# Half of the last 1 MB of output weights loaded by a transfer of 125 partitions

## The chip, the cores and the metric

The kernel runs on one core of one Trainium2 chip. The metric is device time in microseconds (us) of that core. Repeated runs of one kernel agree within about 0.2%.

## The reference

One decode step of a transformer block, batch 8, one token each: layer norm with modulation from a conditioning vector `c`, grouped-query attention over a cache of 8192 keys (32 query heads, 8 key/value heads of 128), output projection, and a squared-ReLU MLP.

```python
def _A_ref(x, k_cache, v_cache, wq, wo):          # x: 8 x 1 x 512
    q = (x @ wq).reshape(B, Sq, Hq, Dh)...         # 32 heads of 128
    scores = einsum('bhqd,bhkd->bhqk', q, k) * Dh ** -0.5
    o = einsum('bhqk,bhkd->bhqd', softmax(scores), v)
    return o.reshape(B, Sq, Hq * Dh) @ wo          # wo: 4096 x 512
...
x = x + ga * _A_ref(h, A_k_cache, A_v_cache, A_wq, A_wo)
h = _layernorm(x) * (1 + cb) + sb
x = x + gb * _B_ref(h, B_w1, B_b1, B_w2, B_b2)
```

Keys and values are 268 MB of bf16. Everything else is small: `wo` is 4 MB.

## The kernel before

A helper records operations per engine and adds the semaphores. All large loads are issued from SyncE into one queue. Four ring slots of 4 MB take two key or value heads each; a slot is loaded again when its reader is done.

```python
def load(n):                                   # 64 loads of 4 MB, 128 partitions x 32 KB
    ...
    loaded[n] = dma("sync", s_ring[s], lambda e: e.dma_start(slot(s), src), dep)
...
load(0)
load(1)
...                                            # b1, b2
wo_e = wo_sb[:, 0:24, :].rearrange("p (g j) n -> p g (j n)", j=4)
d_woe = dma("sync", s_woe, lambda e: e.dma_start(
    wo_e, A_wo[0:24 * DH, :].rearrange("(g p j) n -> p g (j n)", g=6, p=128)))   # 3 MB, rows of 4 KB
d_wo = dma("sync", s_wo, lambda e: e.dma_start(
    wo_sb[:, 24:32, :], A_wo[24 * DH:, :].rearrange("(h dh) n -> dh h n", dh=DH)))  # 1 MB, rows of 1 KB
load(2)
load(3)
...                                            # 8 batches: transpose keys, scores, softmax, values
```

At the very end `w1` (two transfers) and `w2` (four) are loaded by the same queue into a free ring slot, behind the last values. The last matmuls of the MLP wait for the last of them.

Of the kernel before, what the change touches and what calls it, by code (L numbers as in the profile page):

```python
# [30 lines left out]
class Prog:  # L31
# [27 lines left out]
    def dma(self, eng, sem, fn, deps=()):  # L59
        self.dma_n[sem] = self.dma_n.get(sem, 0) + 16  # L60
        self.ops[eng].append(Op(fn, deps, None, sem, self.at))
        return Tok(sem, None, self.at, self.dma_n[sem])
# [90 lines left out]
def bass_adaLN_cond__gqa_block_cached__dense_activation_squared_relu__decode_kernel(  # L153
    nc, A_x, A_k_cache, A_v_cache, A_wq, A_wo, B_x, B_w1, B_b1, B_w2, B_b2, c, w_mod, out):
    B, _, D = A_x.shape
    _, HKV, SK, DH = A_k_cache.shape
# [14 lines left out]
    with ExitStack() as es:  # L171
# [4 lines left out]
        wo_sb = sb("wo_sb", [128, HQ, D], BF16)  # L176
# [72 lines left out]
        op, dma = Pg.op, Pg.dma  # L249
        sem = lambda name: E(nc.semaphore(name))  # L250
        s_c, s_x, s_wm, s_wq, s_woe, s_wo, s_bb = (
            sem(f"d_{n}") for n in ("c", "x", "wm", "wq", "woe", "wo", "bb"))
# [68 lines left out]
        def load(n):  # L321
            kv, b, p = units[n]
            s = n % NSLOT
            src = (A_k_cache if kv == "k" else A_v_cache)[b, 2 * p:2 * p + 2]
            src = src.rearrange("g s d -> (g s d)").rearrange("(p f) -> p f", p=128)
            dep = [released.get(s)]
            if units[n] == last:
                t0, toks = 0, []
                for i, t1 in enumerate(CH):
                    toks.append(dma("sync", s_last[i], lambda e, a=t0 * DH, z=t1 * DH: e.dma_start(  # L330
                        RING[:, s, a:z], src[:, a:z]), dep))
                    t0 = t1
                loaded[n] = toks
            else:
                loaded[n] = dma("sync", s_ring[s], lambda e: e.dma_start(slot(s), src), dep)
# [54 lines left out]
        for g in range(HKV):  # L390
# [14 lines left out]
        wo_e = wo_sb[:, 0:24, :].rearrange("p (g j) n -> p g (j n)", j=4)  # L405
        d_woe = dma("sync", s_woe, lambda e: e.dma_start(
            wo_e, A_wo[0:24 * DH, :].rearrange("(g p j) n -> p g (j n)", g=6, p=128)))
        d_wo = dma("sync", s_wo, lambda e: e.dma_start(
            wo_sb[:, 24:32, :], A_wo[24 * DH:, :].rearrange("(h dh) n -> dh h n", dh=DH)))
        load(2)  # L410
        load(3)
        next_load = NSLOT
# [68 lines left out]
        for b in range(B):  # L481
# [4 lines left out]
            for p in range(NP):  # L486
                n = 2 * NP * b + p
# [65 lines left out]
            for p in range(NP):  # L553
                n = 2 * NP * b + NP + p
# [180 lines left out]
```

## Time and profile before

| | before |
|---|---|
| time, median (range) | 670.66 us (670.59 to 670.72) |
| span of the profiled run | 668.8 us |
| TensorE busy | 74% |
| DMA busy, by slices | 90% or more in 39 of 40 slices |
| bytes moved | 283.95 MB, 425 GB/s on average |

From the page of before: the busy share of TensorE and of the DMA engines in tenths, in 40 slices of the span, and what the DMA engines moved.

```profile
PE   2394964799639983699647996399846996489976
...
DMA  9999999999999999999999999999999999999996
GB/s 375 430 404 427 431 427 437 434 425 433 433 433 427 432 433 435 431 429 429 435 435 425 434 433 432 427 431 433 439 433 423 428 439 435 421 433 435 437 408 259
```

TensorE has gaps everywhere, the DMA engines have none: the loads set the pace. From the DMA issues of before (size of each, time from issue to landing):

```profile
ring<-in_A_k_cache_dram SPq DMA_DIRECT2D x32, 4096.0 KB, 34.9
...
wo_sb<-in_A_wo_dram SPq DMA_DIRECT2D x1, 3072.0 KB, 45.4
...
wo_sb<-in_A_wo_dram SPq DMA_DIRECT2D x1, 1024.0 KB, 47.9
```

A 4 MB load takes 9.7 us when its turn has come (the distance between successive landings). Key loads land 35 us after their issue, value loads 28 us (medians), so two to three others are queued ahead of each. (SPq is SyncE's queue, which issues the transfers; "issue" is time in which an engine waited for nothing that the profile shows.) The end of the chain of waits of before (start, length, what):

```profile
649.68 1.45 SPq L602
651.13 0.05 issue
651.18 14.19 DMA ring<-in_B_w_dram
665.38 0.05 issue
665.42 0.39 PE PS L685 x8
```

The last slice of `w2` lands at 665.38 us, and about 3.4 us of work follow. Four stretches around the loading of the 1 MB. The columns are the stretch, its length, the busy time and count of PE (TensorE's matmuls), PEld (its weight loads), DVE (VectorE), ACT (ScalarE) and POOL (GpSimd), then the TensorE clock, the busy share of the DMA engines and GB/s.

```profile
44.00:48.00 4.00, 4.00 (x68) 2.94 (x66) 2.58 (x4) 2.72 (x3) 0.00 (x0) 1.00 1.03 394
48.00:52.00 4.00, 4.00 (x70) 3.26 (x71) 2.99 (x5) 2.20 (x4) 0.00 (x0) 1.00 1.16 423
52.00:56.00 4.00, 0.39 (x8) 0.00 (x0) 0.28 (x1) 0.91 (x1) 0.00 (x0) 0.98 1.08 461
56.00:60.00 4.00, 0.00 (x0) 0.00 (x0) 0.00 (x0) 0.00 (x0) 0.00 (x0) 0.50 1.00 426
```

The trace also holds two raw lists that the argument rests on: each DMA packet's start, duration and size (a packet is here one row of a transfer, as in the 8192 packets of 32 KB for 64 transfers of 4 MB; there is no engine number), and the landing records, the semaphore increments of a transfer. Each 4 MB load has 16 of them. They are read here as one from each of the 16 DMA engines as it finishes. Each comes with a packet of 4 bytes (before has 1242 of these in the main queue), so the queue's packet count on a page also tells how many landings there were. The spread of the 16 says how far the engines are out of step.

| last slice of w2 | first engine lands | last engine lands | spread |
|---|---|---|---|
| before | 661.64 us | 665.38 us | 3.74 us |

The last engine is the one that matters. The chain above ends at its landing.

### The profile page before, as it was taken

What the parts mean: (1) busy time and instruction counts of PE and PEld (TensorE: products, weight loads), DVE (VectorE), ACT (ScalarE), POOL (GpSimd) and SP (SyncE); (2) the same over time, 40 slices, a digit from 0 to 9 for tenths busy, and PEclk for the clock granted to TensorE, in tenths of its full rate; (3) what the DMA queues carried; (4) which work ended last, traced back from release to release, by engine and by line L of the source; (5) the groups of instructions that cost most, each with busy time, mean ns of one, the idle gap of its engine ahead of it and who ended that gap; (6) DMA issues with size and microseconds to landing.
All of it is one profiled execution on the core that took longest, in us unless ns stands there. A gap on an engine that the chain in (4) does not pass through costs nothing.

```text
span 668.8 us, 16189 instructions
## 1 busy us (share of the span) xinstructions
PE 495.9 (74%) x7492; PEld 341.4 (51%) x7492; DVE 298.8 (45%) x567; ACT 235.1 (35%) x280; POOL 16.9 (3%) x66
## 2 busy tenths in 40 slices
PE   2394964799639983699647996399846996489976
PEld 2383731676318751477316762287414772167634
DVE  2162741466316661267414672166613673156722
ACT  2061630365106640166204660056402662046600
POOL 7200000000000000000000000000000000000000
PEclk9996995699869997699967997589966999689986
DMA  9999999999999999999999999999999999999996
GB/s 375 430 404 427 431 427 437 434 425 433 433 433 427 432 433 435 431 429 429 435 435 425 434 433 432 427 431 433 439 433 423 428 439 435 421 433 435 437 408 259
DMA packets 12969, 283.95 MB, mean 425 GB/s; under 512 B 1266, under 2 KB 2323, under 8 KB 4372
## 3 DMA queue, kind: packets, MB, share of 16 engines
q1 hardware_dynamic: 12900, 283.65, 99.1%
q8 instruction: 13, 0.21, 0.1%
q14 instruction: 8, 0.07, 0.0%
q10 hardware_dynamic: 48, 0.02, 0.0%
HBM read 283.66 MB, written 0.01 MB: 424 GB/s over the span
## 4 chain that ended last, share of the span: by engine, by line
PE 50%; DMA 39%; DVE 5%; ACT 2%; SPq 2%; issue 1%
DMA ring<-in_A_k_cache_dram 37%; PE PS L429 36%; PE PS L444 9%; DVE Pm L533 3%; PE PS L561 2%; DMA ring<-in_B_w_dram 2%; SPq L602 2%; ACT KTb L434 1%; ACT P_sb L511 1%; DVE m L449 1%; PE PS L520 1%; PE PS L420 1%; PE PS L540 0%; DVE rhs_r L537 0%; DVE Dm L502 0%
## 5 line engine op out<-in xcount | busy, mean ns | idle before, releaser
L434 ACT ACTIVATE KTb<-PS 128x1024 bf16<-128x1024 bf16 x192 | 196.7, 1024 | 375.9 <-PE PS L429 375.9
L429 PE MATMUL PS<-IDENT,ring 128*128 128x128 bf16 x4096 | 267.3, 227 | 51.6 <-DMA ring<-in_A_k_cache_dram 51.6
L429 PEld LDWEIGHTS PS<-IDENT,ring 128*128 128x128 bf16 x4096 | 246.7, 102 | 100.3 <-DMA ring<-in_A_k_cache_dram 53.6
L436 DVE COPY KTb<-PS 128x1024 bf16<-128x1024 bf16 x320 | 210.2, 688 | 151.6 <-PE PS L429 149.2
L561 PE MATMUL PS<-ring,Pm 128*32 128x512 bf16 x992 | 83.3, 495 | 63.2 <-DMA ring<-in_A_v_cache_dram 62.3
L570 DVE CAST O_sb<-PS 128x512 bf16<-128x512 f32 x31 | 21.4, 692 | 144.5 <-PE PS L561 144.5
L444 PE MATMUL PS<-KTb,Qb 128*32 128x512 bf16 x1024 | 79.1, 386 | 4.5 <-ACT KTb L434 4.5
L561 PEld LDWEIGHTS PS<-ring,Pm 128*32 128x32 bf16 x992 | 29.5, 116 | 101.9 <-DMA ring<-in_A_v_cache_dram 63.6
L420 PE MATMUL PS<-IDENT 128*128 128x512 bf16 x120 | 31.3, 380 | 0.0
L574 PEld LDWEIGHTS PS<-SEL,O_sb 128*128 128x128 bf16 x124 | 5.3, 99 | 45.3 <-DVE O_sb L570 45.3
L511 ACT ACTIVATE P_sb<-PS,negm 128x512 bf16<-128x512 f32 x32 | 21.6, 686 | 18.9 <-DVE negm L507 18.9
L574 PE MATMUL PS<-SEL,O_sb 128*128 128x8 bf16 x124 | 8.0, 170 | 24.8 <-DVE O_sb L570 24.8
L444 PEld LDWEIGHTS PS<-KTb,Qb 128*32 128x32 bf16 x1024 | 15.4, 94 | 21.1 <-ACT KTb L434 8.5
L533 DVE COPY Pm<-PS 64x512 bf16<-64x512 bf16 x48 | 19.5, 419 | 13.4 <-PE PS L520 12.4
L449 DVE TENSOR_REDUCE m<-PS 128x1 f32<-128x512 f32 x32 | 22.1, 689 | 6.6 <-PE PS L444 6.6
L520 PE MATMUL PS<-IDENT,P_sb 128*64 128x128 bf16 x512 | 20.4, 222 | 2.0 <-ACT P_sb L511 1.2
L520 PEld LDWEIGHTS PS<-IDENT,P_sb 128*64 128x64 bf16 x512 | 15.2, 109 | 9.8 <-ACT P_sb L511 9.8
L420 PEld LDWEIGHTS PS<-IDENT 128*128 128x128 bf16 x120 | 9.9, 103 | 10.8 <-issue 3.4
L577 DVE TENSOR_TENSOR oTn<-PS,rinv 128x8 bf16<-128x8 f32 x31 | 6.0, 194 | 10.9 <-PE PS L574 10.9
L530 ACT ACTIVATE Pm<-PS 64x512 bf16<-64x512 bf16 x16 | 9.5, 593 | 1.1
L386 PE MATMUL PS<-haT,ring 128*128 128x8 bf16 x128 | 3.6, 168 | 7.6 <-DMA ring<-in_A_wq_dram 7.6
L668 ACT ACTIVATE std<-PS,epst 128x8 f32<-128x8 f32 x1 | 0.3, 268 | 25.1 <-PE PS L667 25.1
(112 smaller groups left out, 98.8 us busy)
## 6 DMA issues: line engine op xcount, KB each, us to landing
ring<-in_A_k_cache_dram SPq DMA_DIRECT2D x32, 4096.0 KB, 34.9
ring<-in_A_v_cache_dram SPq DMA_DIRECT2D x31, 4096.0 KB, 28.2
ring<-in_A_wq_dram SPq DMA_DIRECT2D x1, 4096.0 KB, 20.6
ring<-in_w_mod_dram SPq DMA_DIRECT2D x1, 3072.0 KB, 10.6
wo_sb<-in_A_wo_dram SPq DMA_DIRECT2D x1, 3072.0 KB, 45.4
ring<-in_A_v_cache_dram SPq DMA_DIRECT2D x1, 2048.0 KB, 23.6
ring<-in_B_w_dram SPq DMA_DIRECT2D x3, 512.0 KB, 17.5
ring<-in_B_w_dram SPq DMA_DIRECT2D x1, 1344.0 KB, 21.1
```

What stands on the lines that cost most here:

```text
L420: op("tensor", lambda e: e.matmul(bank(at).rearrange("p (a r) -> p a r", a=4), IDENT[:, :], rhs))
L429: t = op("tensor", lambda e, j=j, i=i: e.matmul(STG[j][:, i, :], src[:, 32 * k + 8 * j + i, :], IDENT[:, :], is_transpose=True), [loaded[n ...
L434: stg_free[j] = op("scalar", lambda e, j=j, dst=dst: e.activation(dst, STG[j], ACT.Copy), [t], "scaP")
L436: stg_free[j] = op("vector", lambda e, j=j, dst=dst: e.tensor_copy(dst, STG[j]), [t], "vecP")
L444: t = op("tensor", lambda e, hf=hf, q=q, rhs=rhs: e.matmul(PS[32 * q:32 * (q + 1), k, :], Qb[:, 2 * p + hf, :], rhs, start=(p == 0 and hf ...
L449: return op("vector", lambda e: e.tensor_reduce(m4[:, k:k + 1], bank(k), AX.X, ALU.max), [t])
L511: exps.append(op("scalar", lambda e, k=k: e.activation(P_sb[:, k, :], bank(k), ACT.Exp, bias=negm[:, 0:1], scale=inv_sqrt, accum_out=rs4[: ...
L520: t = op("tensor", lambda e, k=k, i=i, hf=hf, src=src: e.matmul(STG[k][64 * hf:64 * (hf + 1), i, :], src, IDENT[:, :], is_transpose=True, ...
L533: done.append(op("vector", lambda e, dst=dst, frm=frm: e.tensor_copy(dst, frm), [t, k_pm], "vecP"))
L561: t = op("tensor", lambda e, p=p, m=m, cg=cg, vt=vt, Obank=Obank: e.matmul(Obank[32 * cg:32 * (cg + 1), :], lhs[:, p, 32 * m:32 * m + 32], ...
L570: t = op("vector", lambda e, osb=osb, Obank=Obank: e.tensor_copy(osb, Obank), [t], "vecP")
L602: d_w2 = [dma("sync", s_w2[i], lambda e, a=a, z=z, j=j: e.dma_start(W2v[:, a:z, :].rearrange("p (k j) n -> p k (j n)", j=j), B_w2[128 * a: ...
```

## The change

The intent is to move work between DMA engines: half of the 1 MB (four of eight heads) is loaded by a transfer that only some of the engines carry, so that the others have less to do.

```diff
-        d_wo = dma("sync", s_wo, lambda e: e.dma_start(
-            wo_sb[:, 24:32, :], A_wo[24 * DH:, :].rearrange("(h dh) n -> dh h n", dh=DH)))
+        wo_l = A_wo[24 * DH:, :].rearrange("(h dh) n -> dh h n", dh=DH)
+        for p0, p1, h0, h1 in ((0, 125, 0, 4), (125, 128, 0, 4), (0, 128, 4, 8)):
+            d_wo = dma("sync", s_wo, lambda e, p0=p0, p1=p1, h0=h0, h1=h1: e.dma_start(
+                wo_sb[p0:p1, 24 + h0:24 + h1, :], wo_l[p0:p1, h0:h1, :]))
```

## The prediction

How many engines carry a transfer of 125 or of 3 partitions: I took 5 and 3. No record has engine numbers: "engines 0 to 4" is my name, here and in the expectations, for the five that carry the 125 partitions, and "5 to 15" for the other eleven. That the 3 partitions fall on three of the five (132 to 136 packets) is my assumption. The lead of 0.5 us of the slowest of the five rested on such numbers. I took a depth of about 64 packets per engine at which SyncE's issues block.

The forecast's sum came to 3.4 (the middle of 3.1 to 3.7) - 0.5 = +2.9 us, or 673.5 us. The 0.5 stands in it as my estimate, not shown by the trace. The 1.9 us of the other engines is no term of that sum, since they "gain nothing". Its 36 is the 100 packets of the 125-partition transfer less 64, and its 4 the packets per engine of the 3-partition transfer. The runs don't give one depth: in before, SyncE's issue of the 1 MB lasted from 4.07 to 23.16 us, and with the packets counted off at that time, about 63 per engine were queued ahead of it when the issue ended. The four issues of w2 ended with 61 to 65 ahead, but that of load 2, at 44.89 us, with about 80.

On the steps of the spread, in before: it grew from 2.14 us for the load that lands from 89 us on to 3.42 us for the next, where fetch packets of 16 KB (1.02 us each) began at 88.5 and 98.8 us, and from 3.51 to 3.97 us between the loads from 516 and 526 us, where a fetch packet of 8 KB took 0.32 us at 521 us.

> **What bounds the kernel now.** The DMA engines. The page gives them 90% or more busy in 39 of 40 slices; the table by stretches 1.00 busy at 432 GB/s from 62 to 640 us. TensorE is busy 74% and, in the list of waits, idle mostly for key and value tiles. Loads land 26 to 39 us after issue although one 4 MB load takes 9.7 us: the queues are never empty before the end. The landing records of the trace (16 semaphore increments per load, one per engine) show the engines out of step: a load's increments spread over 2.0 us when the output weights land, 3.4 us at 113 us, 3.7 to 4.0 us at the end, growing in steps at instruction-fetch packets of 16 KB (about 1.1 us each). As no engine catches up, the slowest engine's total work sets the end: the last slice of w2 lands at 664.3 us, the last 24 matmuls wait for it 0.42 us.
>
> **What the change does.** [...] The trace shows no engine numbers[...].
> Packets of 1 KB take 48 ns median in the packet records. Before, each engine has 64. After, engines 0 to 4 have 132 to 136, engines 5 to 15 have 32. So engines 0 to 4 get 68 to 72 x 46 to 51 ns = 3.1 to 3.7 us more, the others 32 x 48 = 1.5 us less. Total bytes are unchanged. Two more issues on SyncE (0.4 us each) are hidden.
>
> **Does the relief count?** Only if all of engines 0 to 4 were over 3.5 us ahead of the last. At the end, ten engines land 2.4 to 3.7 us before the last, six 0 to 1.7. [...] Then the end moves by about 3.4 - 0.5 = +2.9 us.
> Second, the relief is partly lost at once: [...] The 100-packet transfer fills the queues of engines 0 to 4, later transfers are held behind it, so the other engines run dry for about (36+4) x 48 ns = 1.9 us near 46 to 48 us of the span, and gain nothing.
>
> **Prediction.** 673.5 us, range 671.6 to 676.0. Faster by over 2%: 0.01, within 2%: 0.975, slower by over 2%: 0.015.
>
> **What would show it.**
> - Landings from load 2 on: five of 16 increments about 3.3 us later against the rest; spread over 4.5 us after wo, 5.5 to 7 at the end.
> - A dip of DMA share in the slice of 45 to 52 us.
> - Chain of waits: still DMA at the end, w2's last landing near 667 us, the same 4.5 us tail.
> - Compute busy times unchanged.
>
> **What would make it wrong.** If engines 0 to 4 are all early ones, the cost is only +0.5 to +1; if their writes contend with others' partitions, packets take longer and the cost reaches 5 us; if later instruction fetches fall on other engines, +-1.5 us.

## The result

| | before | after |
|---|---|---|
| time, median (range) | 670.66 us (670.59 to 670.72) | 676.31 us (676.03 to 676.98) |
| span of the profiled run | 668.8 us | 675.1 us |
| last slice of w2, first engine lands | 661.64 us | 664.54 us |
| last engine lands | 665.38 us | 671.70 us |
| spread | 3.74 us | 7.15 us |
| 1 KB packets of wo, mean | 50.6 ns | 73.5 ns |

The ratio is 1.0086, with a 95% interval of 1.0068 to 1.0103: the change costs 5.65 us by the medians. A ratio here is the mean time of one kernel's fast runs over that of the other's of the same rounds, so it is not quite the ratio of the medians. The prediction was 673.5, range 671.6 to 676.0: the direction and kind were right, the size was half of the measured one, and the time lies just outside the range.

The same lines of the page of after:

```profile
PE   2391984699639994599747996299936996479976
...
DMA  9999999999999999999999999999999999999995
GB/s 374 431 363 377 432 427 434 431 433 431 431 431 433 426 431 433 433 433 435 431 433 433 430 429 428 433 431 433 435 433 431 431 431 431 429 433 429 433 411 198
```

The third and fourth slices (34 to 68 us) fell from 404 and 427 GB/s to 363 and 377; afterwards the rates are as before. But the busy share in tenths is as high as before in both of these slices: the engines were occupied, with less moved. The four-microsecond stretches of after show it more sharply:

```profile
44.00:48.00 4.00, 4.00 (x68) 2.94 (x66) 2.82 (x5) 2.71 (x3) 0.00 (x0) 1.00 0.90 326
48.00:52.00 4.00, 4.00 (x71) 3.46 (x68) 2.67 (x5) 2.40 (x3) 0.00 (x0) 1.00 1.15 275
52.00:56.00 4.00, 0.71 (x11) 0.12 (x8) 0.60 (x2) 1.02 (x1) 0.00 (x0) 1.00 1.02 269
56.00:60.00 4.00, 0.00 (x0) 0.00 (x0) 0.00 (x0) 0.00 (x0) 0.00 (x0) 0.59 1.05 436
```

Only the first has a clearly lower busy share (0.90 against 1.03). In the next two the engines are nearly as busy as before (1.15 and 1.02 against 1.16 and 1.08) and move 275 and 269 GB/s against 423 and 461; the fourth moves as much as before. This is mostly not idling. It is packets that take longer: the packet records of after have the loads' 32 KB packets at 1846 ns on average from 47 to 56 us, 2595 ns at most, against a median of 1218 ns in the steady stream of before. The end of the chain of after:

```profile
654.19 16.88 DMA ring<-in_B_w_dram
671.07 0.05 issue
671.11 0.59 PE PS L687 x16
671.70 0.04 issue
671.74 0.39 PE PS L687 x8
```

The last landing is 6.32 us later, and the span is 6.3 us longer; what follows the landing is the same. (The profiled run of after was its slowest, 676.98.) The landing records split these 6.32 us in two: the first engine to finish is 2.90 us later, and the spread is 3.41 us larger. The prediction had the second part (3.4 us for engines 0 to 4) and held the first to be zero. The split shows at once: the 16 landings of load 2 lie at 59.7 to 61.7 us in before; in after eleven lie at 62.7 to 63.7 us and five at 66.1 to 68.0. Against the mean of before (60.6 us) the eleven are about 2.5 us later and the five about 6.2.

The sum of all packet durations of the main queue grew with the same bytes: 10604.4 us before, 10650.3 after. Over 16 engines that is 2.9 us more per engine on average. (That the first engine is also 2.90 us later is no check of this sum: the mean of the last slice's 16 landings is 3.65 us later. The other 0.8 us fit the lower busy share of the three stretches: 0.13, 0.01 and 0.06 of 4 us.)

The DMA issues of after show the three transfers:

```profile
ring<-in_A_k_cache_dram SPq DMA_DIRECT2D x32, 4096.0 KB, 34.6
...
wo_sb<-in_A_wo_dram SPq DMA_DIRECT2D x1, 3072.0 KB, 46.2
...
wo_sb<-in_A_wo_dram SPq DMA_DIRECT2D x1, 512.0 KB
wo_sb<-in_A_wo_dram SPq DMA_DIRECT2D x1, 500.0 KB
...
wo_sb<-in_A_wo_dram SPq DMA_DIRECT2D x1, 12.0 KB
```

Their shared semaphore has 26 records. That is 5 + 3 + 16 landings and one immediate increment for each of the two transfers on fewer engines (at 23.2 and 46.7 us, when their issues end), which agrees with 5, 3 and 16 engines. The main queue has 12908 packets against 12900 in before, the 5 + 3 landings more.

### The profile page after: what moved, and what is told of

It reads as the page before. It is cut to its first block, busy times and chain, and to the rows that moved or that the text cites. A ratio compares the mean times of both kernels' runs of the same rounds, so it can differ in the third digit from the quotient of the medians.

```text
span 675.1 us, 16191 instructions
## 1 busy us (share of the span) xinstructions
PE 494.9 (73%) x7492; PEld 341.5 (51%) x7492; DVE 298.3 (44%) x567; ACT 235.0 (35%) x280; POOL 16.9 (3%) x66
## 3 DMA queue, kind: packets, MB, share of 16 engines
q1 hardware_dynamic: 12908, 283.65, 98.6%
## 4 chain that ended last, share of the span: by engine, by line
PE 52%; DMA 38%; DVE 5%; ACT 2%; SPq 1%; issue 1%
PE PS L431 38%; DMA ring<-in_A_k_cache_dram 36%; PE PS L446 10%; DVE Pm L535 3%; DMA ring<-in_B_w_dram 2%; PE PS L563 2%; ACT KTb L436 1%; SPq L604 1%; ACT P_sb L513 1%; DVE m L451 1%; PE PS L522 1%; PE PS L422 1%; PE PS L542 0%; DVE rhs_r L539 0%; DVE Dm L504 0%
## 5 line engine op out<-in xcount | busy, mean ns | idle before, releaser
L563 PE MATMUL PS<-ring,Pm 128*32 128x512 bf16 x992 | 81.0, 484 | 64.2 <-DMA ring<-in_A_v_cache_dram 63.3
L579 DVE TENSOR_TENSOR oTn<-PS,rinv 128x8 bf16<-128x8 f32 x31 | 6.0, 193 | 10.9 <-PE PS L576 10.9
```

What stands on the lines that cost most here:

```text
L563: t = op("tensor", lambda e, p=p, m=m, cg=cg, vt=vt, Obank=Obank: e.matmul(Obank[32 * cg:32 * (cg + 1), :], lhs[:, p, 32 * m:32 * m + 32], ...
```

## The experiments

Three theories. **C**: the packets of the 125-partition transfer meet those of the loads where they are written, so both take longer. **S**: the other engines stand dry while the transfer, with 100 packets for each of five engines, fills these engines' queues. **N**: only unequal load, at 48 ns per packet. The table is read from the landing and packet records of each profiled run; "packet time" is the summed duration of the main queue's packets over 16, against before.

| run | time, median | first / last landing of w2's last slice | spread | packet time per engine | 1 KB packets, mean |
|---|---|---|---|---|---|
| before | 670.66 | 661.64 / 665.38 | 3.74 | 0 | 50.6 ns |
| after | 676.31 | 664.54 / 671.70 | 7.15 | +2.9 us | 73.5 ns |
| split | 670.66 | 661.82 / 665.35 | 3.53 | +0.1 us | 50.5 ns |
| pieces | 676.58 | 662.99 / 671.15 | 8.16 | +2.5 us | 54.8 ns |
| rows4k | 676.21 | 663.39 / 671.00 | 7.61 | +2.9 us | 75.6 ns |
| one_head | 671.96 | 661.72 / 666.66 | 4.94 | +0.5 us | 57.8 ns |
| equal112 | 672.59 | 663.45 / 667.32 | 3.87 | +2.0 us | 75.4 ns |
| half_left_out | 669.36 | 660.20 / 664.01 | 3.81 | -1.7 us | 49.5 ns |

The durations of packets overlap (the busy share from 48 to 52 us of before reads 1.16), so the sums are good for differences only.

### split: two transfers of 128 partitions

```diff
-        for p0, p1, h0, h1 in ((0, 125, 0, 4), (125, 128, 0, 4), (0, 128, 4, 8)):
+        for p0, p1, h0, h1 in ((0, 128, 0, 4), (0, 128, 4, 8)):
```

> Control: the same 1 MB in two transfers, both of 128 partitions, so all 16 engines have their 64 packets of 1 KB as before. All theories: the time of before (670.7 us, +-0.5), 1 KB packets at 48 ns median; one issue more on SyncE costs nothing.

Measured 670.66 us (670.56 to 670.79), ratio 1.000 (0.998 to 1.002). Cutting the transfer in two costs nothing. What costs is the 125 + 3 partitions.

### pieces: the same, head by head behind later loads

```diff
+        pieces.update({2: (0, 125, 0, 1), 3: (0, 125, 1, 2), 4: (0, 125, 2, 3),
+                       5: (0, 125, 3, 4), 6: (125, 128, 0, 4)})    # load(n) issues piece n behind load n
+        wo_piece(0, 128, 4, 8)
```

> The same 125-partition work, but head by head (25 packets per engine) behind loads 2 to 5, so that no transfer is held up behind a full queue. Theory C (the end is set by engines 0 to 4, whose own 104 packets run slowly because they meet the others' writes): the dip of DMA throughput near 50 us goes, but the end stays at +5 to +7.5 us (675.7 to 678), 1 KB packets of the pieces at 75 to 100 ns, 32 KB packets beside them longer than 1217 ns. Theory S (the other engines standing dry costs the time): the end falls to +2 to +3.5 us (672.7 to 674.2). Theory N (48 ns per packet as predicted, rest starvation): +3.4.

Measured 676.58 us (676.31 to 677.00), ratio 1.0089. The stretches of this run:

```profile
44.00:48.00 4.00, 4.00 (x68) 2.94 (x66) 2.59 (x5) 2.41 (x3) 0.00 (x0) 1.00 1.02 395
48.00:52.00 4.00, 4.00 (x68) 2.93 (x65) 3.04 (x5) 2.50 (x3) 0.00 (x0) 1.00 1.16 472
52.00:56.00 4.00, 0.06 (x4) 0.00 (x0) 0.00 (x0) 0.57 (x1) 0.00 (x0) 0.93 1.07 453
56.00:60.00 4.00, 0.00 (x0) 0.00 (x0) 0.00 (x0) 0.00 (x0) 0.00 (x0) 0.50 1.04 373
```

The dip of 44 to 56 us is gone, and the busy share of these stretches is above 1. The time did not come back. So the dry queues (S) were not what set the end: they cost the average engine about 0.8 us in after (above) and none here (its 16 last landings are 2.57 us later on average, with 2.5 us more of packet time), but the last engine lands nearly as late (671.15 against 671.70 us). One detail missed: the pieces' own packets took about 60 ns, not the 75 to 100 expected. The cost sits in the loads beside them: while the first piece is in flight, the 32 KB packets of the other engines lengthen from 1214 ns to at most 1707 ns.

### rows4k: neighbouring rows, packets of 4 KB

```diff
+                d_wo = dma("sync", s_wo, lambda e, p0=p0, p1=p1: e.dma_start(
+                    wo_sb[p0:p1, 24:28, :].rearrange("p j n -> p (j n)"), wo_r[p0:p1, :]))   # wo_r: (p j) n -> p (j n)
```

> Wrong result on purpose: the 125-partition transfer reads neighbouring rows, so 25 packets of 4 KB per engine in place of 100 of 1 KB, to the same partitions; no queue fills. If the writes to other engines' partitions are what is slow (C, destination): 4 KB packets at 230 to 290 ns instead of 160, the others' packets still near twice as long, end +4 to +6 us. If the scattered 1 KB rows of the source are what is slow: 4 KB packets at 160 to 170 ns, 25 x 162 = 4.1 us against 32 x 50 = 1.6 us, end about +2 to +2.5 us.

The four heads' rows end up on the wrong partitions. The result still passed the comparison, as the attention term is small beside x, so a pass shows little about this part. Measured 676.21 us (676.14 to 676.27), ratio 1.0082. 156 packets of 4 KB took over 200 ns, on average 276 ns (the transfers have 128; the rest are of the 3 MB still in flight beside them); in before the mean of the 4 KB packets after 50 us was about 160 ns. The scattered 1 KB rows of the source, and the number of packets, are not the cause. With 25 packets per engine the busy share did not drop from 44 to 48 us either (1.03, as before), which speaks against S a second time.

### one_head: a quarter of the dose

```diff
-        for p0, p1, h0, h1 in ((0, 125, 0, 4), (125, 128, 0, 4), (0, 128, 4, 8)):
+        for p0, p1, h0, h1 in ((0, 125, 0, 1), (125, 128, 0, 1), (0, 128, 1, 8)):
```

> A quarter of the dose: one head of eight by 125 + 3 partitions, seven by 128. Engines 0 to 4 have 25 + 1 + 56 = 82 packets of 1 KB instead of 64. With slow packets (75 to 95 ns for the 26): +26 x 85 - 8 x 50 = +1.8 us for these engines; with 48 ns: +0.9 us. The end moves by that less the lead that the slowest of engines 0 to 4 had. If engines 0 to 4 had no lead (the last engine of before is among them): 671.6 (48 ns) or 672.5 (slow). With a lead of 0.5 us: 671.1 or 672.0.

Measured 671.96 us (671.76 to 672.17), ratio 1.0019 (1.0002 to 1.0036): +1.3 us. It lies at the slow case with a lead of 0.5 us (672.0), and 0.4 us above the most that 48 ns allows (671.6). Instruction fetches took up to 1.11 us each in before and 1.26 us in after, and no record says which engine one falls on; on another engine than in before, it could shift the end. So this speaks against 48 ns but does not prove it wrong. It does show that even a small dose costs.

### probe: transfers by themselves, from rest

```python
for name, load in PHASES:            # T: the small transfer; then 4 MB into ring slot 3; then wait for both
    e.dma_start(*T[name]()).then_inc(s_t, 16)
    if load: e.dma_start(RING[:, 3, :], big()).then_inc(s_l, 16)
    ...                              # wait_ge on both
```

> Wrong output on purpose: transfers alone, in phases that wait for one another; most are a small transfer T and a 4 MB load right behind it. Phases: load, load, 128 partitions + load, 125 partitions alone, 125 + load, 125 in 4 KB rows + load, 125 with neighbouring 1 KB rows + load, [...]5 neighbouring partitions alone and + load, 61 partitions[...] alone and + load, 124[...], 104[...], 120[...], 112 alone and + load[...], 64[...], 125 + load, load. Destination theory: 1 KB packets 48 ns when alone[...], 70 to 110 ns with 125, 124, 61 and 112 partitions beside a load, and the load's 32 KB packets then up to twice 1217 ns; 5 neighbouring partitions far slower[...]. Source theory: neighbouring rows bring 125 partitions to 48 ns[...].[...]

The output is wrong in both probes. Two findings. The 250 packets of the 125-partition transfer take 46 ns on average when nothing else runs: the transfer as such is not slow. And the 5 neighbouring partitions 0 to 4 take 6.3 us for 250 KB, where partitions 0, 4, 8, 12 and 16 take 2.8 us for the same bytes. The rest of this probe is inconclusive: a load begun from rest has long first packets even with nothing beside it (its first 16 took 1732 to 1979 ns on average in the three phases with a load alone). My expectation had overlooked this. Also, in the phases of 5 partitions neighbouring rows were joined into packets of 50 KB. Hence the second probe.

### probe2: transfers into a running stream

Each phase is now a load, T, a load, a load in one queue, then a wait. All T have packets of 1 KB.

```python
T = [(T2[:, 0:25, :], wl[:, 0:25, :]),            # 128 partitions
     (T2[0:125, 0:1, :], wl[0:125, 0:1, :]),      # 125, one head
     (T2[0:20:4, 0:50:2, :], rows),               # partitions 0, 4, 8, 12, 16
     (T2[4:24:4, 0:50:2, :], rows),               # 4, 8, 12, 16, 20
     (T2[64:84:4, 0:50:2, :], rows),              # 64, 68, 72, 76, 80
     (T2[0:5, 0:50:2, :], rows),                  # 0 to 4
     (T2[0:61, 0:1, :], wl[0:61, 0:1, :]),
     (T2[0:112, 0:4, :], wl[0:112, 0:4, :]),
     (T2[0:125, 0:4, :], wl[0:125, 0:4, :])]
```

(1) to (9) are the transfers of this list, in its order. The group theory is C with the partitions taken in groups. Which partitions form a group, and which engine writes it, is not shown; these were my assumptions.

> Wrong output on purpose. The first probe's loads began from rest, where packets are long anyway, so each phase now has a load, T, a load, a load in one queue: T meets a running stream. T of 1 KB packets: (1) 128 partitions, 25 rows; (2) 125 partitions, one head; (3) 5 partitions[...], 25 rows; [...](6) 5 neighbouring partitions; (7) 61 partitions[...]; (8) 112 partitions; (9) 125 partitions, four heads. Group theory[...]: in (1) and (3) 46 to 50 ns and the loads' packets at 1214 to 1230 ns; in (2), (4), (5), (9) 55 to 90 ns and the loads' packets up to 1.4 to 2 times longer; in (5) only five engines' loads if the groups are independent, all eleven if the hold-up spreads; (6) slowest. Count theory (the slow packets come with transfers on few engines): (3), (4), (5) alike and slow, (8) fast.

From the packet records ("loads beside" are the 32 KB packets that overlap T; their mean includes those that had nearly ended):

| T | T's packets, mean | loads beside, mean / longest |
|---|---|---|
| 128 partitions | 50 ns | 1253 / 1284 ns |
| 125, one head | 58 ns | 1378 / 1635 ns |
| 0, 4, 8, 12, 16 | 46 ns | 1213 / 1213 ns |
| 4, 8, 12, 16, 20 | 49 ns | 1232 / 1726 ns |
| 64, 68, 72, 76, 80 | 69 ns | 1507 / 2019 ns |
| 0 to 4 | 109 ns | 2008 / 3324 ns |
| 61 | 56 ns | 1331 / 1491 ns |
| 112 | 60 ns | 1410 / 1636 ns |
| 125, four heads (as in the change) | 58 ns | 1793 / 3185 ns |

The third to sixth rows decide. Each is 125 packets of 1 KB, the same rows of the source written to five partitions, and only the partitions differ. Written to 0, 4, 8, 12 and 16, T disturbs nobody and is not disturbed: 46 ns, and 1213 ns for the loads beside it. Written to 64, 68, 72, 76 and 80, T takes 69 ns and the loads' packets 1507 ns on average, 2019 at most; written to 0 to 4, T takes 109 ns and the loads' packets 2008 and 3324 ns. The 112-partition row is slow too (60 ns, 1410 ns), although all 16 engines carry such a transfer (the packet count of equal112, below). So it is neither the number of packets nor their size, nor only that few engines are at work, but which partitions a transfer writes. (Each row is one event in one run; the differences are far larger than the spread of 1213 to 1284 ns in the first and third rows.) In the fourth row four of the five partitions are those of the third, and only one load packet was held up by much (1726 ns).

What stays open: why these partitions and not those. C has T's packets meet those of the loads where they are written, which fits, but no record says which engine writes which partition. And in the fifth row all eleven engines that were carrying loads had packets of 1.6 to 2.0 us. How a hold-up spreads no run here shows.

### equal112: equal load, other partitions

```diff
-        for p0, p1, h0, h1 in ((0, 125, 0, 4), (125, 128, 0, 4), (0, 128, 4, 8)):
+        for p0, p1, h0, h1 in ((0, 112, 0, 4), (112, 128, 0, 4), (0, 128, 4, 8)):
```

> The half is loaded by 112 + 16 partitions: all 16 engines have 28 + 4 = 32 packets of it, as many as before[...]. Unequal load only[...]: the time of before, 670.7. Group theory: the second probe's 112-partition phase lengthened the loads' packets by 7.5 us and its own 448 packets by 12 ns each, 5.4 us, together 12.9 us over 16 engines: +0.8 us, 671.5 (671.1 to 672.0), 1 KB packets at 55 to 62 ns mean.

Measured 672.59 us (672.18 to 673.32), ratio 1.0029 (1.0015 to 1.0043). The end of its chain:

```profile
650.67 16.01 DMA ring<-in_B_w_dram
666.68 0.05 issue
666.73 0.59 PE PS L687 x16
667.32 0.04 issue
667.36 0.39 PE PS L687 x8
```

The main queue has 12932 packets against 12900 in before: 32 landings more, 16 for each of two more transfers, so all 16 engines carry the 112 partitions and the 16. The spread stayed (3.87 against 3.74 us), but all engines finish later, by 1.7 to 2.1 us in order of landing. This isolates a cost that does not come from unequal load, which N has at zero. It is over twice my estimate of 0.8 us. I had left out the transfer of the 16 remaining partitions; that it makes up the difference was not tested.

### half_left_out: 32 packets less for every engine

```diff
+        pool(lambda e: e.memset(wo_sb[:, 24:28, :], 0.0))
...
-            wo_sb[:, 24:32, :], A_wo[24 * DH:, :].rearrange("(h dh) n -> dh h n", dh=DH)))
+            wo_sb[:, 28:32, :], A_wo[28 * DH:, :].rearrange("(h dh) n -> dh h n", dh=DH)))
```

> Wrong result on purpose: half of the 1 MB is set to zero on GpSimd instead of loaded, so every engine has 32 packets of 1 KB less and nothing else changes. If the end follows the DMA work of the last engine one for one: 32 x 48 to 50 ns = 1.5 to 1.6 us less, 669.1 us (668.8 to 669.4). If the end were set elsewhere (TensorE's chain): 670.3 or more.

Its output is wrong, which doesn't matter for the time. Measured 669.36 us (669.07 to 669.53), ratio 0.9980 (0.9966 to 0.9994): 1.3 us less, within the range. The last landing is 1.37 us earlier. The end does follow the DMA work of the last engine, about one for one.

No run beat the kernel before with a right result, and none suggests a version that would.

## Why the prediction was wrong

- **The bound was right.** The DMA engines hardly rest, the last engine sets the end, and what follows the last landing is unchanged. half_left_out confirms it. (The landing of `w2` given as 664.3 us is a slip in a clock offset; the chain has 665.38.)
- **Fewer engines carry it: right.** The 26 records of after agree with 5, 3 and 16.
- **Unequal load: the difference right, in part by luck.** Predicted about 3.3 us for five engines against the others and a spread of 5.5 to 7 us at the end; measured 3.7 us between the five late and the eleven other landings of load 2, and 7.15 us at the end. But both groups came later than predicted, about 6.2 and 2.5 us after the mean of before instead of 3.4 and 0. Longer packets delayed both by a similar amount, so their difference hid the error.
- **The step that failed is the packet time**: "Packets of 1 KB take 48 ns", so "engines 0 to 4 get 68 to 72 x 46 to 51 ns = 3.1 to 3.7 us more, the others 32 x 48 = 1.5 us less". The 48 ns were measured in a transfer of 128 partitions. After the change the mean was 73.5 ns. The five engines began their 132 to 136 packets at 57.3 to 57.6 us of the packet records' clock (10.9 us ahead of the span's); four of them ended at 66.6 to 67.0 and one at 68.7, about 9.7 us on average, 72 ns each. Before, the 64 packets took about 3.0 us, so they got 6.7 us more, not 3.1 to 3.7. The loads of the other engines were slowed as well. Instead of a relief of 1.5 us, the first engine finished 2.90 us later, and packet time rose by 2.9 us per engine. The prediction named this as what would make it wrong ("if their writes contend with others' partitions"), but left it out of the sum.
- **The other engines running dry for 1.9 us**: the dip was there, but it was mostly slow packets. The busy share fell by 0.13, 0.01 and 0.06 in three stretches of 4 us, about 0.8 us in all. pieces removed the dip and kept the time.
- **A lead of 0.5 us** of the slowest of the five: roughly consistent, 6.7 - 6.3 = 0.4 in the profiled run and 6.7 - 5.65 = 1.05 by the medians. The records, which have no engine numbers, do not allow a better figure. An instruction fetch of 1.26 us at 61.2 us may be what held up the one that ended at 68.7.

What the sum lacked is that in these runs a packet's time depended on what ran beside it (125 partitions: 46 ns alone in probe, 58 ns into a stream in probe2) and on the partitions it wrote. The stream of before moved 432 GB/s from 62 to 600 us with the DMA engines 1.00 busy. After the change the engines were nearly as busy from 48 to 56 us (1.15 and 1.02 against 1.16 and 1.08), but moved 275 and 269 GB/s against 423 and 461. And in probe2 125 packets of 1 KB took 46 ns at partitions 0, 4, 8, 12 and 16, with 1213 ns for those of the loads, but 69 ns and up to 2019 ns at 64, 68, 72, 76 and 80. What sets these partitions apart, and how a hold-up spreads to the loads of all eleven engines, the runs do not show.

## What to carry to other kernels

When a stream of 128-partition loads already fills the DMA engines, as here, don't count on relief from moving work between engines by another partition count. Here the eleven engines that were to gain 1.5 us landed load 2 about 2.5 us later than the mean of before, and in probe2 transfers of 61, 112 and 125 partitions took 56 to 60 ns per 1 KB packet, against 50 ns for 128 partitions, and lengthened the packets of the loads beside them to 1331 to 1793 ns on average, against 1253. In such a stream keep transfers at 128 partitions. A count that keeps all 16 engines at work, such as 112 + 16, still cost 2.0 us here for half a megabyte. Before costing moved work with a packet's measured duration, ask whether the packet will still run beside the same neighbours.
